# Value products of a block in one stretch, scores in single banks, sum and division one block later

## The chip, the cores and the metric

The kernel runs on one core of one Trainium2 chip. The metric is the device time of one execution in microseconds; what is compared is the median over several runs. The engines of the core are named as in the profile: PE (TensorE, matrix multiplications), DVE (VectorE), ACT (ScalarE), POOL (GpSimd) and SP (SyncE, which here only issues DMAs). PE's results go to PSUM, eight banks of 128 x 512 fp32; everything else lies in SBUF.

## The reference, cut to what matters

Attention over four batches, eight heads, 768 positions, 64 columns per head, in which a query sees only the keys of its own hash bucket (six sign bits), and behind it a feed-forward part with a three-tap convolution over the positions:

```python
q_bits = (np.einsum('bhsd,dk->bhsk', q, proj) > 0).astype(np.int64)
k_bits = (np.einsum('bhsd,dk->bhsk', k, proj) > 0).astype(np.int64)
mask = q_bucket[:, :, :, None] == k_bucket[:, :, None, :]
scores = np.where(mask, scale * np.matmul(q, k.transpose(0, 1, 3, 2)), -1000000000.0)
scores = scores - np.max(scores, axis=-1, keepdims=True)
attn = np.exp(scores)
attn = attn / (np.sum(attn, axis=-1, keepdims=True) + 1e-09)
x = np.matmul(attn, v)            # heads side by side: 768 x 512
...
h = np.maximum(x @ w_in, 0.0)     # 512 x 1024
conv_out += conv_w[k][None, None, :] * hp[:, k:k + S, :]     # k = 0, 1, 2
gate = 1.0 / (1.0 + np.exp(-conv_out))
return (h * gate @ w_out).astype(np.float32)                 # 1024 x 512
```

## The kernel before

**Units of work.** A pair is two heads of one batch; 16 pairs, four per batch. A pair is worked in two blocks, each half of the queries (384 and 384; in the last pair of a batch 416 and 352). The first block of a pair carries two extra columns for a mean of v. Keys are taken in six chunks of 128.

**One chunk of a block.** `scores` (L322) computes, for each head, keys by queries with two matmuls (L328 with 97 rows, L329 with 128): q and k are split into a high and a low part, R holds q and k as loaded, `hi` the high parts, and after `low` (L223) R holds the low parts. Rows 64 to 95 of KA and QA carry the hash bits as products of large numbers, which makes the mask; row 96 carries the maximum. Both heads go to one PSUM tile of two banks, and one Exp on ACT (L331) turns it into p. `values` (L339) multiplies p by v in fp32, the two heads in the two 64-column halves of the array, and accumulates over the six chunks in one bank. `add` sums p over the chunks, on POOL (L354) and, for the last chunk, on DVE (L352). `sums` (L364) adds that up over the partitions with a matmul by ones; `invert` and `divide` (L371 to L388) divide; `out_high` (L391, ACT) and `out_low` (L395, DVE) split the result x for the feed-forward part. In batch 0 the block is "direct": the last chunk is not added on DVE, and `sums` takes it as a second operand.

**What a pair prepares for others.** Twelve `peak`s (L277, L280) find the maxima of the next pair: PE computes scores into a two-bank tile, DVE reduces it. `turn`, `shift_away` and `shift_back` bring these maxima through DRAM to row 96 of QA. For the pair after next, `hash` (L205), `bits_up` (L211, L214), `high` (L219, ACT), `low` (L223, POOL), `place_a` (L229 to L232) and `place_b` (L237, L238) prepare the operands; the placing is done by DMAs on SP's queue. There is one R buffer, so the load of the next R (L193, in `bring`) waits until `place_b(1)` has read the one before.

**Order.** All instructions are issued in the order of the program text, and each engine works through its own in that order. A pair has six steps (L549): step i takes two chunks, two or three peaks (tables `PEAKS`), then the value products of the step before (`ready`), and, by the age of a block, its sum, its division and its output. So the value products of a pair stand in six places. PSUM: three two-bank tiles S0 to S2 in turn for peaks, scores, hash and sums (`two_banks`), and two single banks for the value products, M0 and M1. In the feed-forward part a `room` gives S2's banks to `hidden` (L406), whose bank i is 2 or 3 in turn for the first four and then one of three; `output` (L431) accumulates in S0 and S1 and copies out (L437). Before it has finished, `ahead` computes the first scores of the next batch. In batch 0 the weights are decoded besides (L110 to L133 on ACT, DVE and POOL).

Of the kernel before, what the change touches and what calls it, by code (L numbers as in the profile page):

```python
# [7 lines left out]
F32 = mybir.dt.float32  # L8
# [25 lines left out]
DEC = ((1, 2), (1, 0), (1, 2), (1, 1), (1, 0), (1, 2))  # L34
DEC_0 = ((0, 0), (0, 0), (1, 1), (1, 2), (1, 0), (1, 2))
PEAKS = (0, 3, 2, 2, 3, 2)
PEAKS_0 = (3, 3, 3, 3, 3, 3)
PEAKS_4 = (0, 3, 3, 2, 2, 2)
FLOOR = float(15 * 2 ** 29)
EARLY_Q, EARLY_K = 384, 512  # L40
HASH = 3
# [5 lines left out]
def lsh_attention_conv_ffn(ctx, tc, qk, v, hw, w_in, conv_w, w_out, consts, ident_in, out):  # L47
# [14 lines left out]
    rooms = []  # L62

    def room(name):

        if rooms:
            rooms.pop()[0].__exit__(None, None, None)
        if name:
            c = tc.tile_pool(name=name, bufs=1, space=PSUM, reuse_waits="tile")
            rooms.append((c, c.__enter__()))  # L70

    def two_banks(name, k=None):

        if k is None:
            k = turns["S"] = (turns.get("S", -1) + 1) % 3
        pool = rooms[0][1] if k == 2 else ps
        return pool.tile([P, 2, 512], F32, tag=f"S{k}", name=name, bufs=1)

    def one_bank(name, k):
        return (ps if k < 2 else rooms[0][1]).tile([P, 512], F32, tag=f"M{k}", name=name, bufs=1)  # L80
# [64 lines left out]
    fetched, decoding, steps, pending = [], [iter(())], [9], []  # L145
# [9 lines left out]
    def spare_bank(name):  # L155
        return one_bank(name, (turns.get("M", 1) + 1) % 2)

    def decode_next():
        decode_on(16)
        steps[0] = 0  # L160
        raw, name = fetched.pop(0)
        decoding[0] = split_weight(raw, name, spare_bank(f"d{name}"))
# [8 lines left out]
    def decode_on(n=1):  # L171
        for _ in range(n):
            next(decoding[0], None)
            steps[0] += 1


    class Pair:
# [21 lines left out]
        def hash(self):  # L199
            hp = two_banks(f"hash{self.nm}")[:, 0, :]  # L200
# [39 lines left out]
        def prepare_now(self):  # L240
# [3 lines left out]
            for h in range(2):  # L244
                hps.append(ring(ps, 2, [P, 512], F32, "M", f"hash{nm}_{h}")[:, :HS])
# [42 lines left out]
        def shift_now(self, t0, n, h):  # L288

            tp = two_banks(f"mt{self.nm}_{t0}_{h}")  # L290
            for j in range(n):
                c = self.column(t0 + j, h)
                nc.tensor.matmul(tp[96:, h, j * P:(j + 1) * P], self.stat[h][:, c:c + 32], ident,
                                 start=True, stop=True, tile_position=(0, 96))
            nc.scalar.copy(self.QA[96:97, h, t0 * P:(t0 + n) * P], tp[96:97, h, :n * P])
# [16 lines left out]
    class Block:  # L312
        def __init__(self, pair, j):
# [6 lines left out]
            self.direct = pair.b == 0  # L320

        def scores(self, c):  # L322

            pr, n = self.pair, self.n
            sp = two_banks(f"s{self.nm}_{c}")[:, :, :n]
            ks, qs = slice(c * P, (c + 1) * P), slice(self.c0 + self.w + 2 - n, self.c0 + self.w + 2)
            for h in range(2):
                nc.tensor.matmul(sp[:, h], pr.KA[:97, h, ks], pr.Q[0][:97, h, qs], start=True, stop=False)  # L328
                nc.tensor.matmul(sp[:, h], pr.KB[:, h, ks], pr.Q[1][:, h, qs], start=False, stop=True)  # L329
            self.pts.append(ring(wp, NPT, [P, 2, WMAX + 2], F32, "big", f"p{self.nm}_{c}")[:, :, :n])  # L330
            nc.scalar.activation(self.pts[c], sp, AF.Exp, scale=SCALE)  # L331

        def values(self, c):

            pr = self.pair
            if c == 0:
                self.av = ring(ps, 2, [P, 512], F32, "M", f"v{self.nm}")[:, :self.n]
            for h in range(2):
                nc.tensor.matmul(self.av[h * D:(h + 1) * D], pr.v[:, c, h, :], self.pts[c][:, h],  # L339
                                 start=(c == 0), stop=(c == NCK - 1), tile_position=(0, h * D))  # L340

        def add(self, c):
# [5 lines left out]
            last = self.j == 1 and self.pair.p == NP - 1 and not self.direct  # L348
            eng = nc.vector if c > DADD - last else nc.gpsimd
# [6 lines left out]
        def sums(self, bank=None):  # L356
            w = self.w
            if bank is None:
                bank = two_banks(f"sum{self.nm}")[:, 0, :]
            self.sm = bank[:, :w]  # L360
# [6 lines left out]
        def invert(self):  # L367
            w = self.w
            self.tt = ring(wp, EB, [P, 2, WMAX], F32, "e", f"r{self.nm}")
            rec = ring(wp, 2, [P, 16], F32, "rec", f"rec{self.nm}")[:, :w // 32]  # L370
            nc.vector.transpose(self.tt[:, 0, :w], self.sm)  # L371
            total = self.tt[:, 0, :w].rearrange("p (j r) -> p j r", r=32)[:, :, 0]
# [4 lines left out]
            self.rec = rec  # L377

        def divide(self):
            w, pr = self.w, self.pair  # L380
            if self.j == 0:
                pr.x = [ring(wp, NP, [P, S], F32R, f"x{k}", f"x{k}{pr.nm}") for k in "hl"]
                pr.mean = ring(wp, 2, [P, 1], F32, "mean", f"mean{self.nm}")
                nc.vector.tensor_scalar(pr.mean, self.av[:, 0:1], 1e-9 / S, None, ALU.mult)
            nc.vector.transpose(self.tt[:, 1, :w].rearrange("p (j r) -> p j r", r=32),
# [318 lines left out]
```

## Time and profile before

| | us |
|---|---|
| median of 3 runs (729.66 to 730.57) | 730.04 |
| the profiled execution | 731.41 |
| its span | 729.6 |
| PE busy | 697.1 |
| DVE busy | 483.4 |
| POOL busy | 389.1 |
| ACT busy | 354.9 |

The profile is one execution. Busy times are sums over the whole span; a timeline row gives start, duration and what the engine waited for in brackets; matmul rows overlap, since the next one starts before the one before has drained, so the distance between starts is what one costs. The granted clock was 0.99 of full speed over the span.

### The profile page before, as it was taken

What the parts mean: (1) busy time and instruction counts of PE and PEld (TensorE: products, weight loads), DVE (VectorE), ACT (ScalarE), POOL (GpSimd) and SP (SyncE); (2) the same over time, 40 slices, a digit from 0 to 9 for tenths busy, and PEclk for the clock granted to TensorE, in tenths of its full rate; (3) what the DMA queues carried; (4) which work ended last, traced back from release to release, by engine and by line L of the source; (5) the groups of instructions that cost most, each with busy time, mean ns of one, the idle gap of its engine ahead of it and who ended that gap; (6) DMA issues with size and microseconds to landing.
All of it is one profiled execution on the core that took longest, in us unless ns stands there. A gap on an engine that the chain in (4) does not pass through costs nothing.

```text
span 729.6 us, 10037 instructions
## 1 busy us (share of the span) xinstructions
PE 697.1 (96%) x3584; PEld 504.4 (69%) x3584; DVE 483.4 (66%) x759; ACT 354.9 (49%) x582; POOL 389.1 (53%) x265
## 2 busy tenths in 40 slices
PE   6999998978999999999999999999999999999997
PEld 3666564666886666568987666668898666658896
DVE  5798986799626877866444778786443777646442
ACT  5545444555444354545444445355444444455443
POOL 7677875756425866742224666852222767552221
PEclk9999999999999999999999999999999999999999
DMA  7757658480102666753012367565011276100011
GB/s 218 183 158 210 148 163 218 103 255 0 44 1 74 153 143 165 162 133 81 1 43 67 86 168 170 120 169 130 1 43 49 61 176 148 26 1 1 0 44 43
DMA packets 38357, 75.87 MB, mean 104 GB/s; under 512 B 8312, under 2 KB 16796, under 8 KB 38308
## 3 DMA queue, kind: packets, MB, share of 16 engines
q1 hardware_dynamic: 33940, 74.60, 38.9%
q10 hardware_dynamic: 4368, 0.64, 0.6%
q8 instruction: 28, 0.46, 0.3%
q14 instruction: 21, 0.17, 0.1%
HBM read 29.71 MB, written 9.73 MB: 54 GB/s over the span
## 4 chain that ended last, share of the span: by engine, by line
PE 78%; DMA 6%; POOL 5%; DVE 4%; ACT 4%; issue 2%; SPq 0%; ACTq 0%; POOLq 0%; DVEq 0%
PE o L431 17%; PE h L406 16%; PE v L339 15%; PE m L277 9%; PE s L328 8%; PE s L329 7%; PE sum L364 3%; DMA R<-in_qk 2%; DMA q<-R 2%; PE hash L205 2%; POOL R L223 1%; ACT p L331 1%; POOL ps L354 1%; DVE stat L280 1%; DVE ht L415 1%
## 5 line engine op out<-in xcount | busy, mean ns | idle before, releaser
L331 ACT ACTIVATE p<-s 128x772 f32<-128x772 f32 (+3 forms) x192 | 147.5, 812 | 199.9 <-PE s L329 189.1
L280 DVE TENSOR_REDUCE stat<-m 128x1 f32<-128x772 f32 x192 | 179.2, 950 | 57.4 <-PE m L277 56.7
L354 POOL TENSOR_TENSOR ps<-ps,p 128x768 f32<-128x768 f32 (+2 forms) x93 | 157.0, 1688 | 69.1 <-ACT p L331 55.8
L423 POOL TENSOR_TENSOR g<-ht,g 128x384 fp32r<-128x384 f32 x64 | 64.9, 1015 | 185.4 <-ACT g L422 174.8
L431 PE MATMUL o<-wo,g 128*128 128x512 f32 x576 | 146.1, 399 | 6.9 <-POOL wo L133 6.5
L406 PE MATMUL h<-xh,wi 128*128 128x386 f32 x512 | 144.4, 343 | 6.0 <-DVE ht L419 6.0
L339 PE MATMUL v<-p,v 128*64 128x386 f32 (+3 forms) x768 | 145.2, 499 | 0.0
L328 PE MATMUL s<-q,k 97*128 97x386 f32 (+3 forms) x384 | 133.8, 349 | 2.1 <-ACT osb L437 2.1
L415 DVE SCALAR_TENSOR_TENSOR ht<-h,cw,ht 128x384 f32<-128x384 f32 (+1 forms) x128 | 78.9, 617 | 79.8 <-ACT ht L413 77.5
L329 PE MATMUL s<-q,k 128*128 128x386 f32 (+3 forms) x384 | 130.9, 341 | 0.0
L431 PEld LDWEIGHTS o<-wo,g 128*128 128x128 f32 x576 | 108.2, 190 | 30.8 <-POOL wo L133 9.1
L277 PE MATMUL m<-k,q 96*128 96x386 f32 x384 | 108.6, 376 | 2.7 <-DVE stat L280 1.5
L406 PEld LDWEIGHTS h<-xh,wi 128*128 128x128 f32 x512 | 94.5, 189 | 16.7 <-DVE ht L419 8.8
L277 PEld LDWEIGHTS m<-k,q 96*128 96x128 f32 x384 | 60.9, 189 | 60.0 <-issue 24.6
L354 POOL TENSOR_TENSOR ps<-p,p 128x768 f32<-128x768 f32 (+2 forms) x32 | 61.5, 1922 | 65.7 <-ACT p L331 65.5
L339 PEld LDWEIGHTS v<-p,v 128*64 128x64 f32 x768 | 47.3, 136 | 64.0 <-issue 63.5
L406 PE MATMUL h<-xl,wi 128*128 128x386 f32 x256 | 86.9, 340 | 0.0
L328 PEld LDWEIGHTS s<-q,k 97*128 97x128 f32 x384 | 73.5, 191 | 14.9 <-ACT xh L391 5.4
L329 PEld LDWEIGHTS s<-q,k 128*128 128x128 f32 x384 | 73.4, 191 | 0.2
L418 ACT ACTIVATE ht<-ht 128x384 f32<-128x384 f32 x64 | 33.6, 526 | 55.6 <-DVE ht L415 55.5
L419 DVE TENSOR_TENSOR ht<-h,ht 128x384 f32<-128x384 f32 x64 | 35.6, 556 | 32.5 <-ACT ht L418 32.5
L412 ACT ACTIVATE h<-h 128x386 f32<-128x386 f32 x64 | 30.5, 477 | 53.7 <-PE h L406 53.0
(86 smaller groups left out, 592.1 us busy)
## 6 DMA issues: line engine op xcount, KB each, us to landing
R<-in_qk SPq DMA_DIRECT2D x15, 768.0 KB
v<-in_v SPq DMA_DIRECT2D x16, 384.0 KB
k<-hi SPq DMA_DIRECT2D x16, 384.0 KB
q<-hi SPq DMA_DIRECT2D x16, 384.0 KB
out<-osb SPq DMA_DIRECT2D x24, 256.0 KB
k<-R SPq DMA_DIRECT2D x15, 384.0 KB
q<-R SPq DMA_DIRECT2D x15, 384.0 KB
q<-hi SPq DMA_DIRECT2D x28, 192.0 KB
```

What stands on the lines that cost most here:

```text
L277: nc.tensor.matmul(mp[:, half], self.QA[:96, h, t * P:(t + 1) * P], self.K[0][:96, h, half * HS:(half + 1) * HS + 2], start=True, stop=True)
L280: nc.vector.tensor_reduce(self.stat[h][:, c:c + 1], mp, mybir.AxisListType.XY, ALU.max)
L328: nc.tensor.matmul(sp[:, h], pr.KA[:97, h, ks], pr.Q[0][:97, h, qs], start=True, stop=False)
L329: nc.tensor.matmul(sp[:, h], pr.KB[:, h, ks], pr.Q[1][:, h, qs], start=False, stop=True)
L331: nc.scalar.activation(self.pts[c], sp, AF.Exp, scale=SCALE)
L339: nc.tensor.matmul(self.av[h * D:(h + 1) * D], pr.v[:, c, h, :], self.pts[c][:, h], start=(c == 0), stop=(c == NCK - 1), tile_position=(0, ...
L354: eng.tensor_tensor(self.acc, first if c == 1 else self.acc, pt, ALU.add)
L406: nc.tensor.matmul(hp[:, :HW], w, x[:, c0:c0 + HW], start=(n == 0), stop=(n == 3 * NCC - 1))
L415: nc.vector.scalar_tensor_tensor(t[:, a:z], hp[:, o + k - 1 + a:o + k - 1 + z], cw[:, f, k:k + 1], t[:, a:z], ALU.mult, ALU.add)
L419: nc.vector.tensor_tensor(t, hp[:, o:o + HS], t, ALU.mult)
L423: nc.gpsimd.tensor_tensor(g[:, 1, :], t, g[:, 0, :].bitcast(F32), ALU.subtract)
L431: nc.tensor.matmul(op, l, r, start=(f == 0 and n == 0), stop=(f == NFC - 1 and n == 2))
```

## The change

The tables of steps go. A block is now: `take` of the block before (a copy of its value bank to SBUF on ACT, and the mean), then its six scores with the peaks in an order written as a string, then the sum and division of the block before, then all six value products, then the last add, in the first block of a pair the hash, `high` and `low` for the pair after next, and at the end the outputs of the block before. Scores of one head take one bank and have their own Exp, except in the last pair of all (`wide`). PSUM: S0 and S1 of two banks (peaks, wide scores, outputs of the feed-forward part), three single banks in turn (scores, sums, hash, hidden tiles) and bank 3 for the value products. `out_low` is on POOL.

```diff
-        for h in range(2):
-            nc.tensor.matmul(self.av[h * D:(h + 1) * D], pr.v[:, c, h, :], self.pts[c][:, h],
-                             start=(c == 0), stop=(c == NCK - 1), tile_position=(0, h * D))
+        self.av = one_bank(f"v{self.nm}", 3)[:, :self.n]
+        for c in range(NCK):
+            for h in range(2):
+                nc.tensor.matmul(self.av[h * D:(h + 1) * D], pr.v[:, c, h, :], self.pts[c][:, h],
+                                 start=(c == 0), stop=(c == NCK - 1), tile_position=(0, h * D))
+    def take(self):
+        self.tt = ring(wp, EB, [P, 2, WMAX], F32, "e", f"r{self.nm}")
+        self.xf = self.tt[:, 0, :w]
+        nc.scalar.copy(self.xf, self.av[:, self.n - w:])
...
             for h in range(2):
-                nc.tensor.matmul(sp[:, h], pr.KA[:97, h, ks], pr.Q[0][:97, h, qs], start=True, stop=False)
-                nc.tensor.matmul(sp[:, h], pr.KB[:, h, ks], pr.Q[1][:, h, qs], start=False, stop=True)
-            nc.scalar.activation(self.pts[c], sp, AF.Exp, scale=SCALE)
+                sp = both[:, h] if wide else one_bank(f"s{self.nm}_{c}_{h}")[:, :n]
+                nc.tensor.matmul(sp, pr.KA[:97, h, ks], pr.Q[0][:97, h, qs], start=True, stop=False)
+                nc.tensor.matmul(sp, pr.KB[:, h, ks], pr.Q[1][:, h, qs], start=False, stop=True)
+                if not wide:
+                    nc.scalar.activation(self.pts[c][:, h], sp, AF.Exp, scale=SCALE)
...
-            nc.vector.tensor_tensor(xl, self.xf, xh.bitcast(F32), ALU.subtract)
+            nc.gpsimd.tensor_tensor(xl, self.xf, xh.bitcast(F32), ALU.subtract)
...
+        for j in range(2):
+            prev, blk = blk, both[n][j]
+            wide = not nxt
+            order = "ssssss" if wide else "msmmsmsmmsmsmms" if n == 0 else "smmsmsmsmsm" if pr.p == j == 0 else "msmsmsmsmsms"
+            if prev:
+                prev.take()
+            for kind in order:
+                if kind == "m":
+                    peak()
+                    continue
+                c = len(blk.pts)
+                blk.scores(c, wide and c % 3 < 2)
+                if c <= blk.dadd:
+                    blk.add(c)
+                if c == 2:
+                    rows_back()
+                    if j:
+                        rows_away()
+                    decode_on(16)
+                if j and nx2 and c == 3:
+                    nx2.place_a(slice(0, EARLY_Q), slice(0, EARLY_K))
+                if j and nx2 and c == 5:
+                    nx2.place_a(slice(EARLY_Q, S), slice(EARLY_K, S))
...
+            if prev:
+                prev.sums(one_bank(f"sum{prev.nm}"))
+                prev.divide()
...
+            blk.values()
+            for c in range(blk.dadd + 1, NCK):
+                blk.add(c)
+            if j == 0 and nx2:
+                nx2.hash()
+                nx2.bits_up()
+                nx2.high()
+                nx2.low(0)
+            if prev:
+                prev.out_high()
+                prev.out_low()
+            if j == 0 and nx2:
+                nx2.low(1)
```

PE, before, where the first block of the second pair of batch 2 ends (v_1_0 are its value products, m_2 the peaks of the next pair, hash_3 the hash of the pair after next):

```order
L277 MATMUL m_2_2_0_3787<-k_0_79,q_0_75 128x386 x2
L339 MATMUL v_1_0_3752<-p_1_0_2_3734,v_1_3561 64x386 x2
L339 MATMUL v_1_0_3752<-p_1_0_3_3742,v_1_3561 64x386 x2
L277 MATMUL m_2_2_1_3799<-k_0_79,q_0_75 128x386 x2
...
L277 MATMUL m_2_3_0_3820<-k_0_79,q_0_75 128x386 x2
L205 MATMUL hash_3_3824<-R_3_3700,hw_sb 32x384 x4
L339 MATMUL v_1_0_3752<-p_1_0_4_3775,v_1_3561 64x386 x2
L339 MATMUL v_1_0_3752<-p_1_0_5_3784,v_1_3561 64x386 x2
L277 MATMUL m_2_3_1_3844<-k_0_79,q_0_75 128x386 x2
```

The same place after:

```order
L258 MATMUL m_2_2_1_3979<-k_0_79,q_0_75 128x386 x2
...
L359 MATMUL sum_0_1_3996<-ps_0_1_3807,ones 64x384 x2
L326 MATMUL v_1_0_4005<-p_1_0_0_3912,v_1_3743 64x386 x2
L326 MATMUL v_1_0_4005<-p_1_0_1_3925,v_1_3743 64x386 x2
L326 MATMUL v_1_0_4005<-p_1_0_2_3940,v_1_3743 64x386 x2
L326 MATMUL v_1_0_4005<-p_1_0_3_3955,v_1_3743 64x386 x2
L326 MATMUL v_1_0_4005<-p_1_0_4_3969,v_1_3743 64x386 x2
L326 MATMUL v_1_0_4005<-p_1_0_5_3985,v_1_3743 64x386 x2
L186 MATMUL hash_3_4019<-R_3_3902,hw_sb 32x384 x4
L258 MATMUL m_2_3_0_4041<-k_0_79,q_0_75 128x386 x2
```

The value products stood in groups of two chunks between peaks and scores; now the sum of the block before (sum_0_1), all six chunks and the hash stand together.

POOL, before, in the second block of the same pair (ps_1_1 is its running sum, R_3 the operand of the pair after next):

```order
L354 TENSOR_TENSOR ps_1_1_3837<-p_1_1_0_3810,p_1_1_1_3818 128x2x384
L354 TENSOR_TENSOR ps_1_1_3837<-ps_1_1_3837,p_1_1_2_3853 128x2x384
L354 TENSOR_TENSOR ps_1_1_3837<-ps_1_1_3837,p_1_1_3_3860 128x2x384
L223 TENSOR_TENSOR R_3_3700<-R_3_3700,hi_3_3839 128x768
L354 TENSOR_TENSOR ps_1_1_3837<-ps_1_1_3837,p_1_1_4_3895 128x2x384
L223 TENSOR_TENSOR R_3_3700<-R_3_3700,hi_3_3839 128x768
```

POOL after:

```order
L204 TENSOR_TENSOR R_3_3902<-R_3_3902,hi_3_4028 128x768
L380 TENSOR_TENSOR xl_0_3778<-r_0_1_3906,xh_0_3777 128x384
L204 TENSOR_TENSOR R_3_3902<-R_3_3902,hi_3_4028 128x768
L351 TENSOR_TENSOR ps_1_1_4067<-p_1_1_0_4045,p_1_1_1_4058 128x2x384
...
L351 TENSOR_TENSOR ps_1_1_4067<-ps_1_1_4067,p_1_1_4_4106 128x2x384
L380 TENSOR_TENSOR xl_1_4038<-r_1_0_4035,xh_1_4037 128x384
```

Both subtractions of R moved ahead of the adds of the second block, and the low halves of x stand between them and behind the adds.

DVE, after, at the end of that pair (stat_84 takes the maxima of the pair after next, ps_1_1 is the last add):

```order
L261 TENSOR_REDUCE stat_83<-m_2_5_1_4116 128x1
L281 STREAM_TRANSPOSE side_2_3_4120<-stat_83 128x32
L365 STREAM_TRANSPOSE r_1_0_4035<-sum_1_0_4135 128x384
...
L373 SCALAR_TENSOR_TENSOR r_1_0_4035<-r_1_0_4035,mean_1_0_4039,sum_1_0_4135 128x384
L349 SCALAR_TENSOR_TENSOR ps_1_1_4067<-ps_1_1_4067,p_1_1_5_4122 128x2x384
L261 TENSOR_REDUCE stat_84<-m_3_0_0_4168 128x1
```

The last add stood there before too; the division of the block before now stands in front of it, and the low half of x, which DVE did, is gone.

## Rows read from the trace of the kernel before

**Rows 1.** From the page: busy time, share of the span and instructions of each engine, and the chain of work that ended last, by engine and by line.
```profile
PE 697.1 (96%) x3584; PEld 504.4 (69%) x3584; DVE 483.4 (66%) x759; ACT 354.9 (49%) x582; POOL 389.1 (53%) x265
...
PE 78%; DMA 6%; POOL 5%; DVE 4%; ACT 4%; issue 2%; SPq 0%; ACTq 0%; POOLq 0%; DVEq 0%
```

**Rows 2.** Busy time by stretch: a pair of batch 2, a pair of batch 0, a short stretch inside batch 0, and the start of the feed-forward part of batch 0. Columns: stretch, its length, then busy time (and instructions) of PE, its weight load, DVE, ACT and POOL, the granted TensorE clock, the DMA share, GB/s.
```profile
399.24:424.43 25.19, 25.19 (x138) 15.91 (x140) 18.93 (x27) 11.16 (x16) 17.63 (x11) 1.00 0.38 83
...
91.02:119.77 28.75, 26.52 (x143) 16.45 (x144) 23.44 (x39) 14.03 (x21) 23.98 (x15) 1.00 0.66 171
120.50:124.00 3.50, 3.50 (x16) 1.23 (x14) 0.98 (x2) 0.72 (x1) 0.00 (x0) 0.51 1.02 276
133.00:155.00 22.00, 15.18 (x79) 11.55 (x77) 16.46 (x31) 12.34 (x24) 13.36 (x11) 0.99 0.68 172
```

**Rows 3.** TensorE's timeline inside that pair of batch 2. Columns: start, time, engine, line, operation, names and shapes, number of instructions in the row.
```profile
406.19 0.34 PE L329 MATMUL s<-q,k 128*128 128x384 f32 x1
...
407.08 1.04 PE L277 MATMUL m<-k,q 96*128 96x386 f32 x4
408.05 1.51 PE L339 MATMUL v<-p,v 128*64 128x384 f32 x8
409.39 0.81 PE L364 MATMUL sum<-ps,ones 128*64 128x384 f32 x4
...
413.96 0.44 PE L328 MATMUL s<-q,k 97*128 97x386 f32 x1
414.24 0.34 PE L329 MATMUL s<-q,k 128*128 128x386 f32 x1
414.42 0.34 PE L328 MATMUL s<-q,k 97*128 97x386 f32 x1
...
415.31 0.34 PE L329 MATMUL s<-q,k 128*128 128x386 f32 x1
415.58 1.51 PE L339 MATMUL v<-p,v 128*64 128x384 f32 x8
417.02 0.62 PE L277 MATMUL m<-k,q 96*128 96x386 f32 x2
...
418.90 1.04 PE L277 MATMUL m<-k,q 96*128 96x386 f32 x4
```

**Rows 4.** Groups of instructions of one shape on ACT, DVE and POOL. Columns: line, engine, operation, names, shapes, count, then busy time and mean ns of one, then idle time before them and what ended it.
```profile
L331 ACT ACTIVATE p<-s 128x768 f32<-128x768 f32 x72 | 54.9, 811 | 82.7 <-PE s L329 73.7 <-POOL ps L354 8.7
...
L412 ACT ACTIVATE h<-h 128x386 f32<-128x386 f32 x64 | 30.5, 477 | 53.7 <-PE h L406 53.0
L219 ACT CAST hi<-R 128x768 fp32r<-128x768 f32 x30 | 23.4, 829 | 2.1 <-DMA R<-in_qk 2.0
...
L280 DVE TENSOR_REDUCE stat<-m 128x1 f32<-128x772 f32 x192 | 179.2, 950 | 57.4 <-PE m L277 56.7
...
L354 POOL TENSOR_TENSOR ps<-ps,p 128x768 f32<-128x768 f32 x72 | 121.2, 1684 | 50.8 <-ACT p L331 38.2 <-DVE r L385 10.0
L423 POOL TENSOR_TENSOR g<-ht,g 128x384 fp32r<-128x384 f32 x64 | 64.9, 1015 | 185.4 <-ACT g L422 174.8 <-issue 10.6
L223 POOL TENSOR_TENSOR R<-R,hi 128x768 fp32r<-128x768 f32 x30 | 54.9, 1833 | 0.1
L354 POOL TENSOR_TENSOR ps<-p,p 128x768 f32<-128x768 f32 x24 | 45.6, 1898 | 56.1 <-ACT p L331 55.9
```

**Rows 5.** Timeline of POOL and DVE around two last additions of a block (L352): one issued beside a subtraction of R (L223), one without. Columns as in rows 3.
```profile
414.41 1.83 POOL L223 TENSOR_TENSOR R<-R,hi 128x768 fp32r<-128x768 f32 x1
...
414.59 2.47 DVE L352 SCALAR_TENSOR_TENSOR ps<-ps,p 128x768 f32<-128x768 f32 x1
...
427.59 0.92 DVE L352 SCALAR_TENSOR_TENSOR ps<-ps,p 128x768 f32<-128x768 f32 x1
```

**Rows 6.** ACT's timeline: two Exps of one step.
```profile
406.62 1.52 ACT L331 ACTIVATE p<-s 128x768 f32<-128x768 f32 x2 [1.60 <-PE s L329]
```

**Rows 7.** What PE waited for over the whole run (total us, times, longest), and two of these places in its timeline.
```profile
PE hash L205 <- DMA R<-in_qk: 3.3, 3, 2.2
PE s L328 <- ACT osb L437: 2.1, 3, 0.7
...
220.65 0.44 PE L328 MATMUL s<-q,k 97*128 97x386 f32 x1 [0.70 <-ACT osb L437]
...
328.03 0.34 PE L406 MATMUL h<-xh,wi 128*128 128x386 f32 x1
328.95 0.44 PE L406 MATMUL h<-xh,wi 128*128 128x386 f32 x1 [0.58 <-DVE ht L419]
```

**Rows 8.** The chain of waits in batch 1 from a subtraction of R to the hash that needs the next R (start, us, what), and that hash in PE's timeline.
```profile
294.14 1.80 POOL R L223
...
296.61 5.08 DMA q<-R
...
301.75 6.53 DMA R<-in_qk
...
308.41 0.85 PE L205 MATMUL hash<-R,hw_sb 128*32 128x384 f32 x8 [0.64 <-DMA R<-in_qk]
```

**Rows 9.** PE's timeline in batch 0, at the hash that waited longest for R.
```profile
119.77 0.85 PE L205 MATMUL hash<-R,hw_sb 128*32 128x384 f32 x8 [2.23 <-DMA R<-in_qk]
120.55 1.65 PE L364 MATMUL sum<-ps,ones 128*64 128x416 f32 x4
```

More of the change, by code (lines that the diff above doesn't have):

```diff
@@ L59, in ring, with one_bank @@
         return pool.tile(shape, dtype, tag=f"{tag}{k}", name=name, bufs=1)
[L62 to L70, printed above, removed]
     def two_banks(name, k=None):
         if k is None:
[L75 to L80, printed above, removed]
+            k = turns["S"] = (turns.get("S", -1) + 1) % 2
+        return ps.tile([P, 2, 512], F32, tag=f"S{k}", name=name, bufs=1)
+    def one_bank(name, k=None):
+        if k is None:
+            k = turns["M"] = (turns.get("M", -1) + 1) % 3
+        return ps.tile([P, 512], F32, tag=f"M{k}", name=name, bufs=1)
     ident = cp.tile([P, P], F32, name="ident")
@@ L320, in __init__, with scores @@
             self.direct = pair.b == 0
-        def scores(self, c):
+            self.dadd = DADD - (j == 1 and pair.p == NP - 1 and not self.direct)
+        def scores(self, c, wide=False):
             pr, n = self.pair, self.n
-            sp = two_banks(f"s{self.nm}_{c}")[:, :, :n]
+            self.pts.append(ring(wp, NPT, [P, 2, WMAX + 2], F32, "big", f"p{self.nm}_{c}")[:, :, :n])
             ks, qs = slice(c * P, (c + 1) * P), slice(self.c0 + self.w + 2 - n, self.c0 + self.w + 2)
+            if wide:
+                both = two_banks(f"s{self.nm}_{c}")[:, :, :n]
@@ L347, in add @@
                 self.acc = ring(wp, EB, [P, 2, WMAX], F32, "e", f"ps{self.nm}")[:, :, :self.w]
-            last = self.j == 1 and self.pair.p == NP - 1 and not self.direct
-            eng = nc.vector if c > DADD - last else nc.gpsimd
+            eng = nc.vector if c > self.dadd else nc.gpsimd
             first, pt = (t[:, :, self.n - self.w:] for t in (self.pts[0], self.pts[c]))
@@ L448, in ffn @@
         todo = [(half, f) for half in range(2) for f in range(NFC)]
[L449 to L453 removed]
+        flag = FLAG if b else FLAG_0
         for i in range(len(todo) + flag):
@@ L457, in ffn @@
             if i < len(todo):
-                run.append(hidden(b, *todo[i], xs, bank(i)))
+                run.append(hidden(b, *todo[i], xs, one_bank(f"h{b}_{i}")))
                 next(run[i])
@@ L531, in bring @@
             pairs[n].place_b(0)
-    waiting, live = [], []
     units = [(first, t, h) for t in range(3, NCK) for h in range(2)]
     both = [[Block(pr, j) for j in range(2)] for pr in pairs]
+    turned, gone = [], []
     def peak():
@@ L540, in peak, with rows_away, rows_back @@
         if h and t in (u.cut - 1, NCK - 1) and u is not first:
-            u.turn(0 if t < u.cut else u.cut)
+            t0 = 0 if t < u.cut else u.cut
+            u.turn(t0)
+            turned.append((u, t0, t + 1 - t0))
+    def rows_away():
+        for u, t0, k in turned:
+            u.shift_away(t0, k)
+            gone.append((u, t0, k))
+        turned.clear()
+    def rows_back():
+        for u, t0, k in gone:
+            u.shift_back(t0, k)
+        gone.clear()
+    blk = None
     for n, pr in enumerate(pairs):
@@ L586, in lsh_attention_conv_ffn @@
                 nx2.hash()
                 nx2.bits_up()
-            if not pr.b:
-                for bk in summing:
-                    bk.sums()
-                    bk.invert()
-            for bk in ending:
-                bk.out_low()
-            if ready and ready[0][1] == 0:
-                decode_on(6 - steps[0])
-            for bk, k in ready:
-                bk.values(k)
-            if pr.b == 0:
-                if n == 0 and i == 1:
-                    decoding[0] = decode_taps(cwr, spare_bank("dcw"))
-                if i in (1, 4):
-                    decode_next()
-                    decode_on()
```

168 lines of the change are left out of this document (43 added, 125 removed).

## The prediction

> **What bounds the kernel now.** I read the page first, then the busy time by stretch, then TensorE's timeline inside one pair, then the rows of the engines that feed it. TensorE (PE) is busy 96% of the span and carries 78% of the chain that ended last; DMA carries 6%, POOL 5%, DVE and ACT 4% each [rows 1]. By stretch, one pair of a later batch takes 25.19 us and PE is busy in all of it, while DVE works 18.93, POOL 17.63 and ACT 11.16; a pair of batch 0 takes 28.75 with PE busy 26.52 [rows 2]. So in batches 1 to 3 only fewer PE microseconds help, and every engine but PE has 6 us or more to spare per pair.
>
> Inside the pair, consecutive score matmuls start .18 apart (413.96 and the rows from 414.24 to 415.31). The value products run with fp32 operands in two 64-column halves of the array, and each time PE turns to them and back it pays: the group at 415.58 starts .27 after the matmul before it (.09 too much); eight of its instructions take 1.34 to the next start when a sum of the same kind follows (408.05 to 409.39), but 1.44 when scores or maxima follow (415.58 to 417.02), so leaving costs .10; and the first matmul behind has .28 to its successor (413.96 to 414.24), another .10 [rows 3]. That is .29 per visit; with a little lost by the first pair of instructions of a group I take .31. A pair has six visits. Four maxima matmuls next to each other take .97 from their start to the group behind them (407.08 to 408.05), less the .09 of entering .16 more than 4 x .18; with the one at 418.90 there are two such places per pair.
>
> **The change part by part.**
>
> *Six visits become two.* Per block one stretch now holds the sum of the block before, the six value products, and in the first block the hash of the pair after next. Four visits less x .31 = 1.24, and maxima now alternate with scores, 2 x .16 = .32. That makes 1.5 us per pair, PE's own work 25.2 - 1.5 = 23.7. Twelve pairs in batches 1 to 3: -18.0. Ends: no gain (if PE is then held by others) and -2.0 x 12 = -24.
>
> *The Exp is split.* 192 Exps, 811 ns for 768 columns, become 368 of half the width and 8 whole ones (in the very last pair). The nearest ACT row, 386 columns from PSUM, takes 477 ns [rows 4], and two 768-wide Exps take 1.52 together, .71 after the first start for the second [rows 6]; a half one would stand between .38 and .48 apart. Two per chunk are .76 to .96 of PE's 1.13 per chunk (four scores and one pair of maxima, 6 x .18, and .05). The score of a head now has one bank of three: matmuls .36 + .16 to drain, .09 to ACT's start (scores end 406.53, Exp starts 406.62), Exp .48 [rows 3, 4, 6], and .05 back to PE by my estimate: 1.15. The bank is wanted again 3 x .36 + .41 = 1.49 later. It fits, with .34 left: cost nothing; the cover is gone at 1.49.
>
> *ACT's two casts of the next R.* They take .83 each [rows 4] and now stand, with the copy out and the new copy of the value bank (.48 each by the 477 above), directly in front of the next block's first Exp. If R lands early they lie under the value stretch, where ACT has no Exp; if it lands at its end, they delay the first Exp by some .7, of which .34 is covered. I take .2 per pair, 12 x .2 = +2.4 (ends 0 and .7 x 12 = +8.4).
>
> *The low half of x goes from DVE to POOL, and the subtractions of R go ahead of the adds.* POOL's row with the same width and two SBUF operands is 1015 ns [rows 4]. Take T as a pair's start. The hash ends the first block at T+12.2 (six chunks 6.8, a sum .65 and six value products 4.0, by the 1.34 of eight instructions [rows 3], the hash .78 [rows 9]), so POOL runs the first R subtraction 12.4 to 14.2, x low to 15.2, the second R to 17.1 (1833 each), then the four adds of the second block, 1.90 + 3 x 1.68, to T+24.05. The next pair is due at T' = T+23.7. POOL goes straight on with the next x low (1.0). Now DVE has the last add of the block in front of the next pair's first maxima. In the trace that add takes .92 when POOL is idle (427.59) but 2.47 when it is issued .18 after an R subtraction of 1.83, ending .82 after POOL is done [rows 5]: it does its work only once POOL has finished. So it ends at T+25.05 + .92 = T'+2.3; the first maximum follows to T'+3.2 (950 ns) and frees the two-bank buffer that the third peak wants at T'+2.26. PE stands about 1.05. This occurs where the block before has an x low: from the second pair to the third and from the third to the fourth, 2 x 3 batches = 6, +6.3. From the first to the second no x low stands there, and it costs 0. Ends: 6 x .1 = +.6 (no blocking: add ends T'+1.3, maximum T'+2.2) and twice that, +12.6, if the first to the second pair and the inner blocks pay too.
>
> The Trainium skill ("SBUF — State Buffer", section "Who interferes with whom") says that a DVE instruction with two SBUF inputs and a GpSimd instruction that reads SBUF lock each other out for the whole instruction, whoever came first. The 2.47 against .92 of the rows agrees; by this rule the term is +6.3, without it +.6, and the rule speaks against putting x low on POOL.
>
> *FFN.* A third hidden bank from the start and no copy-out buffer shared with the first score. The waits were DVE's ht before the fourth hidden tile, .92 from start to start where .18 is usual, and the last copy-out in front of the first scores, .70, each once per later batch [rows 7]: 3 x .7 + 3 x .7 = -4.2. Ends 0 and -4.2. FFN 0, which is paced by the decoding of the weights (15.18 of PE in 22.00 [rows 2]), I leave as it is.
>
> *Batch 0.* A full pair takes 28.75, of which PE works 26.52 [rows 2]. PE's share falls by about 1.5; ACT and DVE, with decoding on top (DVE 23.44 of 28.75), and the loads behind it keep back what PE waits today, 2.2, less some .8, and leave 26.5 (ends 25.0 and 28.8). At one place the hash stood 2.23 for R, and behind that the sums ran at a granted clock of .51, the lower level of 1.2 GHz, and took 1.65 instead of .81 [rows 2, 3, 9]; what of it remains lies inside the ends. Three pairs x -2.2 = -6.6; the first pair, whose hash of pair 2 now waits for an R that lands only after the first block, loses about 1.5 (an estimate, somewhat under the 2.23 that a hash stood for R): together -5 (ends +1.5 and -11).
>
> *The chain through DMA.* One R buffer serves all pairs, and the chain shows it: R subtraction 1.80, q<-R 5.08, R load 6.53, hash [rows 8]. In the new order the second placing is issued behind the last scores of the second block, 6.8 after the hash. I put its landing 4.4 further on (an estimate under the 5.08 of q<-R, since its pieces are smaller); then come two issues of .6, q<-R 5.08 and the load of R, here 6.53: 24.0 from hash to hash against 23.7 of PE and the .2 and .5 of waits above. I let it hide; a rival prices it.
>
> Sum: -18.0 + 2.4 + 6.3 - 4.2 - 5 = -18.5. The profiled execution took 731.41, so 712.9; it lies 1.4 above the median of 730.04. Forecast 711.5, written 711.
>
> **The rivals.**
>
> *A. The waits stay away.* If the last add isn't held and the casts hide, 731.41 - 18.0 - 4.2 - 5 - 1.4 gives 703 or a little less. For it: nothing but PE is busy over 76% of a pair. Against it: the 2.47 of the add in [rows 5].
>
> *B. The R loop paces the pairs.* The load of R is started by POOL's second subtraction and q<-R. If that loop takes 1 us longer than PE's pair, or the placing of the k part lands that much behind the first maxima of the next pair, each of 12 pairs loses 1 us more: 711 + 12 = 723. For it: 5.08 + 6.53 of DMA in one chain [rows 8], three hashes that wait for R, 3.3 us in all [rows 7]. Against it: two of the three are in batch 0 and the third, .64 at 308.41 [rows 8], is the only one in the later batches.
>
> *C. ACT's round trip paces the scores (slower).* Place: the three single banks. It decides from a round trip of 1.49, or from two Exps in sequence of 1.13. Each .1 us over it costs .1 on the chunks of 14 pairs that carry maxima, 14 x 12 = 168, or 17 us, so all of the 18.5 is gone at 1.6; at 1.7 the time is 731 + 35 - 18 - 1, about 747. For it: the half-wide Exp isn't in the trace, and 768 columns at 811 against 386 at 477 show that some .14 of each is fixed. Against it: two times .48 is .96, well under 1.13.
>
> *D. It does what it says and gains nothing,* since the six visits were cover for waits that come out elsewhere (maxima on DVE, .95 each, six in 6.6 us of scores, with the whole division in front of the next stretch [rows 4]): 730.
>
> **How the numbers follow.** Forecast .55, with its own range 704 to 721; A .10; B .12 (721 to 728); D .06; C .17. About 0.2%, 1.5 us, is what a measurement of this kernel can tell from no change. Faster is forecast, A and B, .77; same D, .06; slower C, .17. The range 699 to 732 leaves out most of C and little below.
>
> **What would show it.** Right: two groups of 24 value instructions per pair in PE's timeline; a pair of batch 2 near 23.7 to 24.9; the last add at 1.9 or more with PE waiting 1 us on a maximum at the start of the third and fourth pair; no wait for osb or ht. Wrong: score matmuls that wait on ACT's Exp (C), hash or maxima that wait on a DMA (B), a pair at 25 without a named wait (D).

## The result, and the profile after

The changed kernel takes 711.93 us in the median of four runs (710.7 to 713.11), the kernel before 730.18 beside it: ratio 0.975, 95% interval 0.9727 to 0.9774. The forecast was 711. The profiled execution took 713.11, its span is 711.3, 18.3 less than the 729.6 before. The sum came out right, but by luck: two of its parts, batch 0 and batches 1 to 3, were each off by some 6 us, in opposite directions. This table is read from the first score matmul of each batch and the first hidden matmul of the first feed-forward part, in the two traces:

| stretch | before | after | difference | forecast |
|---|---|---|---|---|
| start to the end of batch 0's attention | 133.08 | 134.16 | +1.08 | -5 |
| feed-forward part of batch 0 | 79.69 | 79.75 | +0.06 | 0 |
| batches 1 to 3 | 516.83 | 497.39 | -19.44 | -13.5 |

The first view is the page of the changed kernel: the busy times of the engines and the chain by engine, answering to [rows 1].

```profile
PE 677.7 (95%) x3584; PEld 517.9 (73%) x3584; DVE 475.9 (67%) x727; ACT 388.4 (55%) x798; POOL 420.8 (59%) x297
...
PE 69%; DVE 9%; POOL 9%; DMA 6%; ACT 3%; issue 3%; SPq 1%; ACTq 0%; POOLq 0%; DVEq 0%
```

PE lost 19.4 us of busy time with the same 3584 matmuls, somewhat more than the 18.3 of the span: the work is the same, and what a matmul costs in its place fell. PE's share of the chain fell from 78 to 69%, DVE's and POOL's rose to 9% each.

The second view is the busy time by stretch, as [rows 2]: the second and the third pair of batch 2 (columns as there).

```profile
408.30:432.09 23.79, 23.79 (x138) 16.77 (x137) 18.18 (x26) 13.94 (x31) 18.51 (x13) 1.00 0.66 164
432.09:456.49 24.40, 23.66 (x138) 16.70 (x137) 18.89 (x26) 13.70 (x31) 19.16 (x12) 1.00 0.68 164
```

The pair that took 25.19 takes 23.79, and PE is still busy in all of it. The third has 23.66 of PE and 0.74 of waiting. Where, PE's timeline shows (as [rows 3]); first the end of a block, then the start of the third pair:

```profile
414.69 0.87 PE L359 MATMUL sum<-ps,ones 128*64 128x384 f32 x4
415.39 4.06 PE L326 MATMUL v<-p,v 128*64 128x386 f32 x24
419.38 0.85 PE L186 MATMUL hash<-R,hw_sb 128*32 128x384 f32 x8
420.16 0.62 PE L258 MATMUL m<-k,q 96*128 96x386 f32 x2
...
431.49 0.76 PE L258 MATMUL m<-k,q 96*128 96x386 f32 x2
...
433.71 0.34 PE L314 MATMUL s<-q,k 128*128 128x386 f32 x1
434.79 0.62 PE L258 MATMUL m<-k,q 96*128 96x386 f32 x2 [0.74 <-DVE stat L261]
```

All 24 value instructions stand together and take 3.99 to the hash, .33 per two, where eight alone took 1.44 [rows 3]. The third peak of the pair waits .74 for a maximum. What DVE and POOL did then:

```profile
432.03 1.02 POOL L380 TENSOR_TENSOR xl<-r,xh 128x384 fp32r<-128x384 f32 x1
432.10 1.76 DVE L349 SCALAR_TENSOR_TENSOR ps<-ps,p 128x768 f32<-128x768 f32 x1 [2.15 <-POOL ps L351]
433.78 3.71 DVE L261 TENSOR_REDUCE stat<-m 128x1 f32<-128x772 f32 x4
```

The add on DVE starts .07 behind the low half of x on POOL, takes 1.76 and ends .81 after POOL has finished, as in [rows 5], where it took .92 alone and, beside POOL's 1.83, took 2.47 and ended .82 after POOL. In the list of PE's waits of batches 1 to 3 (total, times, longest) this is all that is left; the waits for osb and ht of [rows 7], and for R of [rows 8], are gone.

```profile
PE m L258 <- DVE stat L261: 3.7, 5, 0.8
```

### The profile page after: what moved, and what is told of

Same layout as the page of the kernel before. It is cut to its first block, busy times and chain, and to the rows that moved or that the text cites. A ratio compares the mean times of both kernels' runs of the same rounds, so it can differ in the third digit from the quotient of the medians.

```text
span 711.3 us, 10277 instructions
## 1 busy us (share of the span) xinstructions
PE 677.7 (95%) x3584; PEld 517.9 (73%) x3584; DVE 475.9 (67%) x727; ACT 388.4 (55%) x798; POOL 420.8 (59%) x297
## 4 chain that ended last, share of the span: by engine, by line
PE 69%; DVE 9%; POOL 9%; DMA 6%; ACT 3%; issue 3%; SPq 1%; ACTq 0%; POOLq 0%; DVEq 0%
PE o L416 18%; PE h L391 17%; PE v L326 9%; PE m L258 7%; PE s L313 7%; PE s L314 6%; POOL ps L351 5%; PE sum L359 3%; DVE stat L261 2%; DMA R<-in_qk 1%; DMA q<-R 1%; DMA top<-side 1%; POOL R L204 1%; DVE ps L349 1%; PE hash L186 1%
## 5 line engine op out<-in xcount | busy, mean ns | idle before, releaser
L316 ACT ACTIVATE p<-s 128x386 f32<-128x386 f32 (+3 forms) x368 | 160.9, 490 | 70.5 <-PE s L314 51.5
L391 PE MATMUL h<-xh,wi 128*128 128x386 f32 x512 | 142.3, 341 | 1.1 <-DVE ht L404 1.1
L326 PE MATMUL v<-p,v 128*64 128x386 f32 (+3 forms) x768 | 129.8, 487 | 0.0
L326 PEld LDWEIGHTS v<-p,v 128*64 128x64 f32 x768 | 54.8, 137 | 68.7 <-issue 67.7
L258 PEld LDWEIGHTS m<-k,q 96*128 96x128 f32 x384 | 68.9, 196 | 35.7 <-issue 15.1
L351 POOL TENSOR_TENSOR ps<-p,p 128x768 f32<-128x768 f32 (+2 forms) x32 | 58.9, 1840 | 47.4 <-ACT p L316 44.5
L204 POOL TENSOR_TENSOR R<-R,hi 128x768 fp32r<-128x768 f32 x30 | 55.0, 1842 | 36.3 <-PE hash L186 26.7
```

Source lines behind the costliest of these rows:

```text
L204: nc.gpsimd.tensor_tensor(R, R.bitcast(F32), self.hi[:, h].bitcast(F32), ALU.subtract)
L258: nc.tensor.matmul(mp[:, half], self.QA[:96, h, t * P:(t + 1) * P], self.K[0][:96, h, half * HS:(half + 1) * HS + 2], start=True, stop=True)
L316: nc.scalar.activation(self.pts[c][:, h], sp, AF.Exp, scale=SCALE)
L351: eng.tensor_tensor(self.acc, first if c == 1 else self.acc, pt, ALU.add)
L391: nc.tensor.matmul(hp[:, :HW], w, x[:, c0:c0 + HW], start=(n == 0), stop=(n == 3 * NCC - 1))
```

## The experiments

Each was timed beside the kernel before on the same chip; "the changed kernel" is the run c0 or its ratio. c0 to e3 ran on one chip, e4 to e9 on another, so for these the ratios are what is compared. The length of batches 1 to 3 in a trace repeats well: 497.4 to 497.7 in the four runs whose code there is that of the changed kernel (c0, e4, e5 and the result's own).

**The changed kernel again** (c0). 

> The changed kernel again, unaltered, as the reference on this chip for the runs beside it. Both theories: 709 to 714 us, five waits of PE for DVE's maxima of 0.6 to 0.8 in batches 1 to 3.

Measured: 713.16, ratio .9757 (.974 to .9775), its batches 1 to 3 take 497.68. It is what the runs of its group are compared with.

**The low half of x one block later** (e1).

```diff
                 if c <= blk.dadd:
                     blk.add(c)
+                if c == 1 and late:
+                    late.pop().out_low()
...
                 prev.out_high()
-                prev.out_low()
+                if j and pr.b and pr.p < NP - 1:
+                    late.append(prev)
+                else:
+                    prev.out_low()
```

> In batches 1 to 3 the low half of x of a pair's first block stays on POOL but is issued one block later, behind POOL's first add of the next pair, so that POOL has nothing to issue beside the last add on DVE. Theory L (the last add is held by POOL's x low, and that makes PE wait): the last add falls from about 1.76 to 0.9 to 1.0 us, the waits of PE for maxima at the start of the third and fourth pair (3.7 us in five) go, 3 to 4 us less than the changed kernel run beside it. Rival (the add is simply late, because POOL's four adds end late): the waits stay within 0.2 of 0.74 each, no gain.

Measured: 710.14, ratio .9714 (.9692 to .9735), 3.0 less than c0. Of PE's waits in batches 1 to 3 only this is left:

```profile
PE hash L186 <- DMA R<-in_qk: 0.6, 2, 0.5
```

The wait for the maxima is gone with nothing moved but one POOL instruction, and the add's median falls from 1.30 to 0.96. So the add was held by what POOL ran beside it; late it was not. But batches 1 to 3 took only 1.6 less (496.06 against 497.68). By the distances between starts in the two traces, the places from scores to peaks lost 3.7, and .7 came back between maxima, .7 before the hash and .7 around the scores. The two profiled executions differ by 2.8; the other 1.2 of that came before batch 1, in code which the edit does not touch, so not all of the 3.0 is the edit's.

**The low half of x on DVE, ahead of the last add** (e2).

```diff
             blk.values()
+            if prev and pr.b:
+                prev.out_high()
+                prev.out_low(nc.vector)
             for c in range(blk.dadd + 1, NCK):
                 blk.add(c)
```

> In batches 1 to 3 the low half of x goes back to DVE, issued ahead of the last add. Theory L: as with the later x low the five waits go (-3.7 us), since POOL is relieved of 2 us per pair and the adds also end 1 us earlier. Rival (DVE is the engine that is short, so more work on it makes the maxima later): the waits stay or grow, 0 to +4 us.

Measured: 708.03, ratio .9691 (.9675 to .9708), 5.1 less than c0 and the fastest version here; batches 1 to 3 take 493.00, 4.7 less. The same two pairs as above:

```profile
406.29:429.91 23.62, 23.62 (x138) 16.73 (x137) 19.65 (x29) 13.79 (x31) 17.42 (x10) 1.00 0.67 167
...
429.91:453.84 23.93, 23.61 (x138) 16.65 (x137) 19.51 (x29) 13.87 (x31) 17.40 (x10) 1.00 0.71 169
```

And what PE still waited for in batches 1 to 3:

```profile
PE hash L186 <- DMA R<-in_qk: 0.8, 3, 0.3
```

DVE works .6 to 1.5 us more per pair than in the changed kernel and PE waits less: DVE was not short, it was held. The .3 that is left in the third pair is the hash standing for R, rival B at its beginning.

**The value stretch cut in two by a peak** (e3, all batches but the first pair; e8, batches 1 to 3).

```diff
             for c in range(NCK):
+                if c == 3 and between:
+                    between()
...
-            blk.values()
+            blk.values(peak if split else None)
+            if split:
+                rows_back()
+                rows_away()
```

> From the second pair on, one peak of each block is taken out of the scores and put between the third and fourth value product, so that each value stretch is entered and left twice: 28 visits more in all, 22 of them in batches 1 to 3. Theory V (a visit costs about 0.33 us beyond its work): +7.3 us in batches 1 to 3, and up to +2 in batch 0, so 7 to 9 us slower than the changed kernel run beside it, unless the later peak takes away some of the waits for DVE (then 4 to 6). Rival (the gain came from setting maxima apart from each other and from waits that went, not from the visits): within 2 us of it.

Measured: 742.68, ratio 1.0157 (1.0135 to 1.018), some 29 slower than the changed kernel: neither theory. In the trace batches 1 to 3 lost 9.6 and the feed-forward part of batch 0 3.0. The attention of batch 0 alone lost 19 (it ends at 153.13 instead of 133.99), about half of it in waits that the edit itself makes: the peak's maximum now stands on DVE behind the division and five decoding operations, and the DMA that sends the maxima off stands at the head of ACT's queue until it has them. The timeline of DVE and ACT:

```profile
87.04 0.95 DVE L261 TENSOR_REDUCE stat<-m 128x1 f32<-128x772 f32 x1
88.03 0.21 DVE L281 STREAM_TRANSPOSE side<-stat 128x32 f32<-128x32 f32 x1
...
88.28 0.54 ACTq L286 DMA_DIRECT2D top<-side  x1
88.86 0.51 ACT L378 CAST xh<-r 128x384 fp32r<-128x384 f32 x1 [6.39 <-DVE side L281]
```

ACT did nothing for 6.39 us, and the Exps behind it came late. In the list of PE's waits in that attention (total, times, longest):

```profile
PE s L313 <- ACT p L316: 7.2, 5, 2.3
```

In the changed kernel this was 1.0, and the waits for maxima there rose from 1.6 to 4.6. How the rest divides between the lower granted clock (.89 from 73 to 105 us, against 1.00 in c0 from 70 to 100) and the visits of batch 0 is not shown. The visit itself is clean in PE's timeline in batch 2 of the same run:

```profile
429.26 2.11 PE L328 MATMUL v<-p,v 128*64 128x384 f32 x12
431.30 0.61 PE L258 MATMUL m<-k,q 96*128 96x386 f32 x2
431.84 2.16 PE L328 MATMUL v<-p,v 128*64 128x384 f32 x12
433.93 0.62 PE L258 MATMUL m<-k,q 96*128 96x386 f32 x2
```

From 429.26 to 433.93 are 4.67; an uncut stretch of this width takes 3.97 (427.52 to 431.49 in the changed kernel) and one peak, two matmuls, .36: that leaves .34 for a visit.

> As the split value stretch before, but in batches 1 to 3 alone, so that the decoding of batch 0 has no part in it: 22 visits more. Theory V (a visit costs 0.34 us beyond its work, as the split stretches of the earlier run show): +7.5 us, and where the peak is missing between two chunks of scores another 0.1 to 0.2 each (2 to 3 us); one or two of the waits for maxima may go (-1): 7 to 11 us slower than the changed kernel. Rival (visits cost nothing, and what the earlier run lost in batches 1 to 3 was disturbance from batch 0): within 2 us.

Measured: 720.99, ratio .987 (.9848 to .9892), 8 slower than the changed kernel by the ratios; in the trace batches 1 to 3 take 508.03, 10.4 more than c0. Theory V holds, and 22 x .34 = 7.5 is its part. The rest are scores of two chunks without a peak between them (two waits for an Exp, 1.9 us in all, and some 40 of .1), while the 3.7 for maxima is gone.

**The first block's late peaks** (e4).

```diff
-            order = "ssssss" if wide else "msmmsmsmmsmsmms" if n == 0 else ...
+            order = "ssssss" if wide else "msmmsmsmmsssmmm" if n == j == 0 else "msmmsmsmmsmsmms" if n == 0 else ...
```

> In the first block of the very first pair the three peaks of the second pair stand behind the last scores instead of between them. Theory F (that block lost time because PE met a peak whose operand was still on its way, 1.57 us, and then worked 3.4 us at the lower clock): the wait and the stretch at the lower clock go, the first pair takes 30 to 31 us instead of 32.9, 2 to 3 us less than the changed kernel. Rival (the operands of the second and third pair come late anyway): the wait moves to the next peaks or to the hash, less than 1 us is gained.

Measured: 712.29, ratio .9751 (.9714 to .9787): no gain, the rival. The 1.57 for the operand is gone, and the hash behind it waits instead in PE's timeline:

```profile
35.57 0.85 PE L186 MATMUL hash<-R,hw_sb 128*32 128x384 f32 x8 [1.61 <-DMA R<-in_qk]
```

The stretches behind it (columns as [rows 2]):

```profile
36.00:40.00 4.00, 3.90 (x20) 3.04 (x13) 2.85 (x5) 2.44 (x5) 3.46 (x2) 0.65 1.02 258
40.00:44.50 4.50, 4.50 (x17) 4.50 (x16) 2.79 (x5) 2.29 (x5) 2.90 (x3) 0.55 0.19 69
```

The lower clock (.65 and .55 in these rows) moved along with the wait; here it lies on more work, and the attention of batch 0 ends 1.1 later than in c0. In either order PE stands for a load in the first pair: in the changed kernel a peak waits for it, here the hash.

**The decoding's scratch in SBUF** (e5).

```diff
-        decoding[0] = split_weight(raw, name, one_bank(f"d{name}", k))
+        bank = one_bank(f"d{name}", k) if k else ring(wp, 2, [P, WC], I32, "wl", f"d{name}").bitcast(F32)
+        decoding[0] = split_weight(raw, name, bank)
```

> The scratch of the weight decoding in the attention of batch 0 lies in SBUF instead of one of the three single banks. Theory D (scores of batch 0 wait for a bank that the decoding holds): the five waits of 0.5 to 0.7 us for the last decoding operation go, 2 to 3 us less up to the end of that attention. Rival (DVE's queue is what is late: the first maxima of a block stand behind the decoding): the waits turn into waits for maxima, less than 1 us is gained, or time is lost where DVE, now with two SBUF operands, meets POOL.

Measured: 729.12, ratio .9988 (.9967 to 1.0009), 16 to 17 slower than the changed kernel; the attention of batch 0 ends 12.1 later than in c0. The bank waits went, as theory D has it, and the rival's last clause decided: DVE now reads two SBUF operands beside POOL. From the timelines of DVE, POOL and PE:

```profile
65.61 0.43 DVE L100 TENSOR_SCALAR di<-wui 128x512 int32<-128x512 int32 x1
...
67.34 2.34 DVE L106 SCALAR_TENSOR_TENSOR wli<-rawi,di 128x512 f32<-128x512 uint32 x1
67.30 1.83 POOL L205 TENSOR_TENSOR R<-R,hi 128x768 fp32r<-128x768 f32 x1 [2.43 <-PE hash L187]
...
69.60 0.60 DVE L193 TENSOR_SCALAR bits<-hash,cst 128x384 fp32r<-128x384 f32 x1
...
70.26 0.69 PE L314 MATMUL s<-q,k 97*128 97x384 f32 x1 [1.47 <-DVE bits L193]
...
82.24 1.46 POOL L381 TENSOR_TENSOR xl<-r,xh 128x384 fp32r<-128x384 f32 x1
82.87 1.12 DVE L100 TENSOR_SCALAR di<-wui 128x512 int32<-128x512 int32 x1
```

The operation with one operand got faster while POOL was idle (.43 against .69 in the changed kernel). The one with two took 2.34 instead of .69 beside a subtraction of R, the bits behind it were late, and PE stood 1.47 and then ran its matmuls .32 apart, at a granted clock of .51 (70.2 to 72 us), the level of 1.2 GHz. In this faster form the operation with one operand was held too: 1.12 beside POOL's low half of x, which itself took 1.46 instead of 1.02.

**All three edits together** (e6). 

> The low half of x on DVE ahead of the last add (batches 1 to 3), the first block's peaks behind its scores, and the decoding scratch in SBUF, together. If the three places are independent: 5.1 us by the first, measured, and 4 to 5 by the two others, 702 to 705 us. If a DMA of R paces the pairs once the waits are gone: 706 or more, with longer waits of the hash for R.

Measured: 723.15, ratio .9886 (.9854 to .9918). This is neither of the two expected times. Batches 1 to 3 take 491.81, 5.9 less than c0, and no hash waits for R there, so no DMA of R paces them. The attention of batch 0, with the scratch in SBUF, ends 14.7 later than in c0 (148.68) and gives back more than that.

**Two banks for the scores instead of three** (e7).

```diff
-                sp = both[:, h] if wide else one_bank(f"s{self.nm}_{c}_{h}")[:, :n]
+                k = h if pr.b and not (self.j == 0 and pr.p == 0) else None
+                sp = both[:, h] if wide else one_bank(f"s{self.nm}_{c}_{h}", k)[:, :n]
```

> In 21 blocks of batches 1 to 3 the scores of a head use two single banks in turn instead of three (sum and hash keep the third). Theory R (a bank is free again 1.15 to 1.19 us after the first matmul of a head, against 1.08 between the uses of one of two banks): some 0.1 us per chunk in 114 chunks, 9 to 15 us slower than the changed kernel. Rival (ACT empties a bank as fast as PE fills the other): within 2 us of it.

Measured: 725.34, ratio .992 (.9883 to .9956), 12 slower than the changed kernel. One chunk and the next, in PE's timeline:

```profile
414.68 0.44 PE L314 MATMUL s<-q,k 97*128 97x386 f32 x1
...
415.94 0.44 PE L314 MATMUL s<-q,k 97*128 97x386 f32 x1
```

1.26 per chunk where three banks give 1.08 (411.71 to 412.79 in the changed kernel), and a pair is back at 25.33. Theory R holds: without the third bank the round trip through ACT eats the whole gain per pair. The lost .18 falls on single starts of .1 each, so the list of PE's waits does not show it.

**Two banks for the first hidden tiles** (e9).

```diff
-                run.append(hidden(b, *todo[i], xs, one_bank(f"h{b}_{i}")))
+                run.append(hidden(b, *todo[i], xs, one_bank(f"h{b}_{i}", i % 2 if b and i < 4 else None)))
```

> In the feed-forward parts of batches 1 to 3 the first four hidden tiles use two single banks in turn, as in the kernel before, and three only from there on. Theory H (the wait of 0.6 to 0.7 us for DVE at the fourth hidden tile of each batch was a bank still in use): three waits of 0.5 to 0.7 us come back, +1.5 to +2.5 us. Rival (that wait went because the value products and sums left that stretch): no change, within 0.5 us in the trace.

Measured: 722.96, ratio .9909 (.9883 to .9935), 11 slower: more than either. The waits of theory H come back at the fourth tile of each of the three parts (324.89, .54). With them come waits that the edit made itself: the third tile waits too (321.97, .83 in each part), and once its fixed banks and the turn of the others meet at a bank that is still in use.

```profile
321.97 0.44 PE L391 MATMUL h<-xh,wi 128*128 128x386 f32 x1 [0.83 <-DVE ht L404]
...
324.89 0.44 PE L391 MATMUL h<-xh,wi 128*128 128x386 f32 x1 [0.54 <-DVE ht L404]
...
658.15 0.44 PE L391 MATMUL h<-xh,wi 128*128 128x386 f32 x1 [3.67 <-DVE ht L404]
```

The waits for ht are 7.8 us in batches 1 to 3, of which the fourth tiles make 1.6, near the 1.7 of the kernel before; and one hash waited 1.9 for R. That the bank is what the fourth tile waited for is shown; the size of the term only nearly, since this edit is not the plain undoing of it.

## Why the prediction was right, and where it was not

**Six visits become two, -18.0: right.** .34 per visit was measured directly against .31, and PE's work in a pair of batch 2 fell from 25.19 to 23.66 and 23.79, against 23.7. In batches 1 to 3, the distances from start to start of all matmuls but the feed-forward part's own, waits left out, sum to 293.6 before, 277.0 after and 275.6 in e2, where nothing waits for maxima: 16.6 and 18.0 less.

**The Exp is split, 0: right.** The half-wide Exp takes 490 ns against the 477 assumed, two of them .88, and no score in batches 1 to 3 waits for one. The cover of .34 was needed: with the bank wanted 1.08 after its first use instead of 1.49, the run with two banks lost 12 us.

**ACT's two casts, +2.4: wrong, 0.** R lands just early enough. In the changed kernel, ACT from the landing to the first Exp, and the matmul that this Exp waits for:

```profile
418.76 1.56 ACT L200 CAST hi<-R 128x768 fp32r<-128x768 f32 x2 [3.44 <-DMA R<-in_qk]
420.23 0.51 ACT L376 CAST xh<-r 128x384 fp32r<-128x384 f32 x1
420.64 0.47 ACT L334 COPY r<-v 128x384 f32<-128x384 f32 x1
421.23 0.87 ACT L316 ACTIVATE p<-s 128x384 f32<-128x384 f32 x2
...
420.79 0.34 PE L314 MATMUL s<-q,k 128*128 128x384 f32 x1
```

The first head's second matmul starts at 420.79 and ends at 421.13; the Exp starts .10 later, the usual distance. Here there was no delay for the .34 to cover, and no wait for ACT stands in the list for batches 1 to 3.

**The last add, +6.3: right in kind and in time, too large by a place.** Count from the first maxima of the pair, as the sum did (431.49 here). The add ended 2.37 later, where the sum had 2.3, and the third peak started at 3.30, where the sum had 3.3 (2.26 and a wait of 1.05). That peak followed the score matmul before it by 1.08 (433.71 to 434.79) instead of .18, so it came .90 late, against 1.05. The list's .74 leaves out the time in which the score matmul still drained. The add's own 1.76 lies somewhat under the 1.9 that the forecast named as a sign. What was wrong is the count: five places, not six. The last pair of all has no peaks, so no maximum is late there; I had counted two per batch in all three. By the list that is 3.7, from start to start 4.5. The rule of the Trainium skill ("SBUF — State Buffer", section "Who interferes with whom"), under which a DVE instruction with two SBUF inputs and a GpSimd instruction that reads SBUF lock each other out, gave the better account: .6 without it, 6.3 with it. That POOL was the cause is shown by e1, which moved one POOL instruction, and by the two-operand decoding of e5.

From the first pair to the second the forecast had no cost, and there was next to none, but its reason was wrong and the number luck. It said that no low half of x stands there; one does, and it holds the add:

```profile
407.43 1.00 POOL L380 TENSOR_TENSOR xl<-r,xh 128x384 fp32r<-128x384 f32 x1
407.50 1.74 DVE L349 SCALAR_TENSOR_TENSOR ps<-ps,p 128x768 f32<-128x768 f32 x1 [1.20 <-POOL ps L351]
```

But the add began .35 before the first maxima of that pair (407.85), not .61 after them, and nobody waited.

**FFN, -4.2: right.** The waits for osb (2.1) and ht (1.7) are gone, -3.8; for ht e9 shows the bank as the cause, for osb no run tried it.

**The DMA chain: right to let it hide.** The hash of batch 1 no longer waits .64. The loop is close, though: a hash waits for R up to .5 in e1, up to .3 in e2 and 1.9 in e9.

With the forecast's -18.0 and the list's waits these terms make -18.0 + 3.7 - 3.8 - .6 = -18.7 in batches 1 to 3; .7 of the 19.4 is not assigned. From start to start the division is another: -16.6 and 3.0 more of waits at the matmuls of the attention, and at the feed-forward part's own -3.8 of waits and -1.8 besides. The value products no longer stand between the hidden tiles there; how much of the 1.8 is theirs was not tried.

**Batch 0, -5: wrong, +1.1.** Three steps of it failed. First, the three full pairs were to lose 2.2 each, 6.6 in all, and lost 4.1: from first score to first score, the last up to the first hidden tile, 27.10, 28.45 and 30.97 became 27.23, 27.36 and 27.84. (In c0 they are 27.47, 28.02 and 26.60, 4.4 less in all, so a single pair says little.) What was missed is a wait that the change makes: the decoding now takes a bank from the three that the scores use, and scores stand behind its last operation. From PE's waits (total, times, longest):

```profile
PE s L313 <- DVE wli L106: 2.6, 5, 0.7
```

That wait is shown; that freeing the bank would gain it is not, since e5 lost more to POOL. Second, the first pair lost 3.1 (29.80 became 32.92) and not 1.5, through a peak whose operand was still on its way and the lower clock behind it. PE's timeline, and then two stretches of one microsecond:

```profile
26.13 0.89 PE L258 MATMUL m<-k,q 96*128 96x386 f32 x2 [1.57 <-DMA q<-far]
```

```profile
27.00:28.00 1.00, 1.00 (x5) 1.00 (x4) 0.94 (x1) 0.30 (x1) 0.48 (x1) 0.50 0.98 227
28.00:29.00 1.00, 1.00 (x4) 1.00 (x4) 0.03 (x2) 0.68 (x2) 0.02 (x1) 0.50 0.24 50
```

PE stood 1.57, then the granted clock read .50, the level of 1.2 GHz. Third, the profiled execution came to its first scores at 18.82 instead of 16.76, which adds 2.1 and, as far as the runs show, is not the change's doing (below). Together -4.1 + 3.1 + 2.1 = +1.1; counted from its first scores, the attention of batch 0 became 1.0 shorter.

**The rivals.** A's time of 703 was not reached, but e2 at 708 lies between it and the forecast. B and C did not happen; e7 showed that C is one bank away. D is excluded by the ratio.

## What to carry to other kernels

Where matmuls of two kinds alternate on PE, count the changes and not the matmuls: here each change there and back cost .34 us. Before moving an elementwise instruction to POOL, look at which instruction on DVE will run beside it and who waits for that one: here those with two SBUF operands were held, and in e5 also the .43 form with one. Where PSUM banks are used in turn, look for a slow user among them: here scores waited 2.6 us for a bank that a decoding step held.

## What was not expected of the hardware

The start-up runs at one of two speeds from execution to execution. In the traces of the changed kernel and its variants the first scores start at 18.65 to 19.07 in eight and at 15.61 or 15.62 in three (e7 to e9), though up to there the code is the same. The same maxima in the changed kernel, and in e9:

```profile
14.37 1.01 PE L258 MATMUL m<-k,q 96*128 96x386 f32 x2 [0.41 <-DVE stat L261]
```

```profile
12.66 0.62 PE L258 MATMUL m<-k,q 96*128 96x386 f32 x2 [0.78 <-DVE stat L261]
```

In the one the first scores start at 18.82, in the other at 15.62, and the attention of batch 0 ends at 134.16 and 130.24. The granted clock of the stretches from 8 to 18 us reads 1.00 in both, so that only the matmuls' own durations show it. For the changed kernel:

```profile
14.00:16.00 2.00, 1.63 (x6) 1.07 (x7) 1.76 (x3) 0.00 (x0) 1.93 (x2) 1.00 0.20 35
```

In the kernel before two such matmuls took the same 1.01 at 15.95, where the granted clock read .50. What decides between the two speeds is open. The 3.2 between the two starts is near the 2.4 that separate the runs of 713.1 and 710.7 us of the changed kernel; that it is the cause there is inferred, since only one of those was profiled. With the quicker start the attention of batch 0 ended 2.2 to 3.0 before the 133.08 of the kernel before (e7 to e9), where the forecast had 5.
